# Second dense layer of three batches by one level of Strassen's method, in a fused attention and dense kernel on one Trainium2 core

## The chip, the cores and the metric

The kernel runs on one core of one Trainium2 chip. The metric is device time in microseconds (us) of one execution, the median of several runs. PE is TensorE, PEld its weight loads, DVE is VectorE, ACT is ScalarE, POOL is GpSimd; SP is SyncE, which issues transfers. In the chains of waits a q behind an engine's name (SPq) is its sequencer, and "issue" is time in which the engine waited for nothing that the profile shows.

Time before the change: 225.6 us median of the first three runs (225.41 to 226.26). Each experiment ran on the same chip as runs of the kernel before in between; x1 to x4, x5 to x8 and x9 to x11 ran on three different chips, where the kernel before had medians of 225.95, 225.98 and 225.92 us.

## The reference

Four batches of windowed attention with four sink tokens (8 heads, 768 tokens, head size 64), then a dense layer of 512 to 2048, relu squared, and a dense layer of 2048 to 512:

```python
scores = np.matmul(q, k.transpose(0, 1, 3, 2)) / np.sqrt(D)
keep = (pos[None, :] < n_sink) | ((rel >= 0) & (rel < window))      # 4, 128
a = softmax(np.where(keep, scores, -1e9))
x = np.matmul(a, v).transpose(0, 2, 1, 3).reshape(B * S, H * D)     # 3072 x 512
h = x @ w_in                                                        # 3072 x 2048
g = np.maximum(h, 0.0) ** 2
return g @ w_out                                                    # 3072 x 512
```

The dense layers are computed in bf16 with f32 sums.

## The kernel before

The kernel is written as operations with a key (a wished-for place), the engines that may run each and an estimated cost. A small planner in the kernel walks them when the program is built, takes the one that can start earliest and, among equals, the one with the smallest key, and emits it. The order on each engine is therefore fixed at build time, out of estimates.

```python
def layer1(b, key, fbs, c0, cw, need):          # first dense layer, relu, square
    ...
    ra = op(key, {"act": 0.19 + n * cw / 1200.0, "dve": 1.25}, relu, after=[a], takes=[rs], reads=[bs])
    def square(e):                              # gT = r * r: two SBUF inputs
        r = bank_t.pop((tag, "r"))
        (nc.vector if e == "dve" else nc.gpsimd).tensor_mul(
            gT_sb[c0 // 512][:, fbs[0]:fbs[0] + n, c0 % 512:c0 % 512 + cw], r, r)
    ops["sq", b, fbs[0], c0, cw] = op(key, {"dve": 0.7}, square, reads=[rs], after=[ra] + ...)

def layer2(b, u, keys, by_part=False):          # second dense layer, a pair of token tiles
    bs, os_ = Slot("den", 1), Slot("osb", 1)    # den: two 2-bank PSUM tiles
    ...
            def mm(e, i=i, t=t, part=part, n=n):
                if n == 0:
                    bank_t["y", b, u] = bank(bs, "py", [128, 2, DM], FP32)     # two PSUM banks
                ...
                for fb in range(4 * part, 4 * part + 4):                       # 16 per tile, 512 columns
                    nc.tensor.matmul(pm[:, i, :], lhsT=gT_sb[t // 4][:, fb, 128 * (t % 4):128 * (t % 4) + 128],
                                     rhs=w_out_sb[:, fb, :], start=(fb == 0), stop=(fb == NFB - 1))
    ...
    def evac(e):                                # one copy when the pair is complete
        o = bank_t["osb", b, u] = work["osb"].tile([128, 2, DM], FP32, name="osb", tag="osb")
        copy(e, o, bank_t["y", b, u])
    # ... one store on the SP queue; the last pair's second tile is copied in two halves, on ACT and DVE
```

A PSUM tile goes back to its pool when its evacuation has read it. Waits between engines are put in by the tile framework, from which instructions touched which tile.

The softmax here doesn't subtract the row's maximum and nothing guards it: scores larger than these inputs give would overflow.

Of the kernel before, what the change touches and what calls it, by code (L numbers as in the profile page):

```python
# [20 lines left out]
WARM_UNTIL = 34.0  # L21

# [10 lines left out]
class Op:  # L33
    def __init__(self, key, engines, run, after, takes, reads, dma, follow):
        self.key, self.engines, self.run = key, engines, run
        self.after, self.takes, self.reads, self.dma = list(after), list(takes), list(reads), dma
        self.follow, self.yields, self.margin = list(follow), [], 0.0
        self.end = self.issued = self.engine = None


class Plan:
# [8 lines left out]
    def __init__(self, capacity):  # L50
        self.ops, self.capacity = [], dict(capacity)

    def op(self, key, engines, run, after=(), takes=(), reads=(), dma=0.0, follow=()):
        o = Op(key, engines, run, after, takes, reads, dma, follow)
        self.ops.append(o)
        return o

    def run(self):
# [12 lines left out]
        while left:  # L71
            best = None
            for o in ready:
                t = 0.0
                need = {}
                for s in o.takes:
                    if len(s.pools) > 1:
                        s.pool = min(s.pools, key=lambda p: min(free[p], default=1e9))
                    need[s.pool] = need.get(s.pool, 0) + 1
                ok = True  # L80
                for p, n in need.items():
                    if len(free[p]) < n:
                        ok = False
                        break
                    t = max(t, sorted(free[p])[n - 1] + LATENCY)
                if not ok:
                    continue
                if o.dma:
                    past = landed.get(next(iter(o.engines)), ())
                    if len(past) >= 8:  # L90
                        t = max(t, past[-8])
                pick = None
                for e, c in o.engines.items():
                    slack = PE_SLACK if e == "pe" else 0.0
                    start = max([t + slack if t > 0 else 0.0, engine.get(e, 0.0)] +
                                [a.end + LATENCY + slack for a in o.after if a.engine != e or a.dma] +
                                [a.issued for a in o.follow])
                    if pick is None or start + c < pick[1] + pick[2]:
                        pick = (e, start, c)
                cand = (round(pick[1], 2), o.key)  # L100
                if best is None or cand < best[0]:
                    best = (cand, o, pick)
# [31 lines left out]
def kernel(  # L134
# [28 lines left out]
    sizes = dict(att=2, den=2, qr=5, qs=6, expm=8, r=3, osb=2)  # L163
# [9 lines left out]
    mask = consts.tile([128, 2, 4, 128], BF16)  # L173
    mask0 = consts.tile([128, 2, 4, 128], BF16)
    bias = consts.tile([128, 4, 128], BF16)
    bias0 = consts.tile([128, 4, 128], BF16)
# [10 lines left out]
    xT_sb = [consts.tile([128, NS, NKB, 256], BF16, name=f"xT{i}") for i in range(2)]  # L187
    gT_sb = [consts.tile([128, NFB, w], BF16, name=f"gT{i}") for i, w in enumerate((512, 256))]
# [63 lines left out]
    def build_masks(e):  # L252
        for h2 in range(2):
            for i in range(2):
                nc.gpsimd.tensor_copy(out=mask[:, h2, 2 * i:2 * i + 2, :], in_=tri)
                nc.gpsimd.tensor_copy(out=mask0[:, h2, 2 * i:2 * i + 2, :], in_=tri)
            nc.gpsimd.memset(mask0[0:NSINK, h2, 1:3, :], 1.0)
# [10 lines left out]
    c_fill = op(-9, {"dve": 2.5}, fill)  # L268
# [11 lines left out]
    def dma_op(queue, name, run, us, behind=None, takes=(), yields=()):  # L280

        def go(e):
            ds = run(e)
            if behind is not None:
                for d in ds:
                    after_dma(d, loaded[behind])
            loaded[name] = ds[-1]
        o = op(-5, {queue: (0.85 if queue == "pool" else 0.5) + (0.3 if behind else 0.0)}, go, dma=us, takes=takes,
               follow=[chained[queue]] if queue in chained else (),
               after=[ops[behind]] if behind is not None else ())  # L290
        ops[name] = chained[queue] = o
        o.yields += [ops[y] for y in yields]
        o.follow += [ops[y] for y in yields]
        return o

# [106 lines left out]
    def attention(b, key):  # L402
# [16 lines left out]
        def stage(g, f0, f1, side):  # L419

# [83 lines left out]
            if g == 0:  # L504
# [7 lines left out]
                def sink_values(e):  # L512
                    for j in range(NP):
# [9 lines left out]
                                    after=([ops["turn", b, 1, 0]] if b in NATURAL else copies) + prev_sinks)  # L523
            lo = max(256, t0)
# [20 lines left out]
            for s in range(t0 // 256, last // 256):  # L545
                fs = 0.36 + 0.5 * (256 * s - t0) / (last - t0)
                norms = []
                biased = b == 0 and s < BIASED
                for m0 in (0, 2):
# [27 lines left out]
                    for ms in ((m0,), (m0 + 1,)) if b == 0 else ((m0, m0 + 1),):  # L577
                        sc.append(op(
                            at(fm), {"pe": len(ms) * (0.7 if biased else 0.28) + 0.1}, lambda e, f=scores, ms=ms: f(e, ms),
                            takes=[banks[m - m0] for m in ms],  # L580
                            after=[ops["turn", b, ti, t] for ti in (0, 1)
# [5 lines left out]
                    for j, m in enumerate((m0, m0 + 1)):  # L587
# [7 lines left out]
                        def domask(e, s=s, m=m, o=o):  # L595
                            x = ex_t[b, s, m]
                            if e == "dve":
                                mk = (mask if s else mask0).rearrange("p h a c -> p h (a c)")
                                nc.vector.tensor_mul(x[:, :, o:512], x[:, :, o:512], mk[:, :, o:512])  # L599
                            elif s == 0:  # L600
                                mk = mask0.rearrange("p h a c -> p h (a c)")
                                nc.gpsimd.tensor_mul(x[:, :, o:512], x[:, :, o:512], mk[:, :, o:512])
# [12 lines left out]
                    bo = Slot(side, 1)  # L615

# [35 lines left out]
                    norms.append(op(at(fm + 0.17), {"dve": 0.95}, norm, after=[va] + prev_bridge, reads=[bo]))  # L652

# [30 lines left out]
    def layer1(b, key, fbs, c0, cw, need):  # L684
        n = len(fbs)
# [14 lines left out]
        def relu(e):  # L700
            r = bank_t[tag, "r"] = work["r"].tile([128, n, cw], BF16, name="r", tag="r")
            if e == "act":
                nc.scalar.activation(out=r, in_=bank_t.pop(tag), func=AF.Relu)  # L703
            else:
                nc.vector.tensor_scalar_max(r, bank_t.pop(tag), 0.0)
# [9 lines left out]
    def layer2(b, u, keys, by_part=False):  # L715

        tail = b == B - 1 and u == NS - 1
        bs = Slot("den", 1)
        bt_ = Slot("den", 1)
# [4 lines left out]
        for n, (i, part) in enumerate(order):  # L724
            t = 2 * u + i

            def mm(e, i=i, t=t, part=part, n=n):
                if n == 0:
                    bank_t["y", b, u] = bank(bs, "py", [128, 2, DM], FP32)
                if tail and n == 4:  # L730
                    bank_t["y", b, u, 1] = bank(bt_, "py", [128, 2, DM], FP32)
                pm = bank_t["y", b, u, 1] if tail and n >= 4 else bank_t["y", b, u]
                for fb in range(4 * part, 4 * part + 4):
# [5 lines left out]
                   takes=[bs] if n == 0 else [bt_] if tail and n == 4 else ())  # L739
# [9 lines left out]
        def store(e):  # L749
            nc.sync.dma_start(out=out[128 * g:128 * g + 256, :].rearrange("(i p) m -> p i m", p=128),  # L750
                              in_=bank_t.pop(("osb", b, u)))

        def evac_tail(i):
            def run(e):
                if i == 0:
                    bank_t["osb", b, u] = work["osb"].tile([128, 2, DM], FP32, name="osb", tag="osb")
                o, y = bank_t["osb", b, u], bank_t["y", b, u] if i == 0 else bank_t["y", b, u, 1]
                if i == 0:
                    copy("dve", o[:, 0, :], y[:, 0, :])
                    nc.sync.dma_start(out=out[128 * g:128 * g + 128, :], in_=o[:, 0, :])  # L760
                else:
                    h = work["qr"].tile([128, DM // 2], FP32, name="half", tag="qr")
                    copy("act", h, y[:, 1, 256:512])
                    copy("dve", o[:, 1, 0:256], y[:, 1, 0:256])
                    nc.scalar.dma_start(out=out[128 * g + 128:128 * g + 256, 256:512], in_=h)
                    nc.sync.dma_start(out=out[128 * g + 128:128 * g + 256, 0:256], in_=o[:, 1, 0:256])
            return run

        if tail:
            e0 = op(keys(0, 3), {"dve": 0.7}, evac_tail(0), after=[ops["layer2", b, 2 * u, 3]], takes=[os_], reads=[bs])  # L770
            op(keys(1, 3), {"dve": 0.5}, evac_tail(1), after=[a, e0], reads=[bt_, os_])
        else:
            ev = op(keys(1, 3), {"act": 1.05, "dve": 1.25}, evac, after=[a], takes=[os_], reads=[bs])
            op(keys(1, 3), {"sp": 0.1}, store, after=[ev], reads=[os_], dma=2.0)
# [32 lines left out]
    for b in range(B):  # L807
        if b == 0:
            at = attention(0, lambda f: f - 1.0)
            at(0, 0.0, 1.0, ("den", "att"))  # L810
            late["masks"] = op(0.006, {"pool": 3.0}, build_masks, after=[c_tri, ops["bridge", 0, 1]])
# [23 lines left out]
        for u in range(NS):  # L835
            if b == 0 and u < 2:
                layer2(b, u, lambda i, part, u=u: 0.408 + 0.466 * (4 * part + 2 * u + i) / 24, by_part=True)
            else:
                layer2(b, u, lambda i, part, u=u, b=b: b + 0.5 + 0.5 * (8 * u + 4 * i + part) / 24)
# [36 lines left out]
```

## Time and profile before

| | before |
|---|---|
| span of the profiled run | 223.8 us |
| PE busy | 215.5 us (96%) |
| DVE, ACT, POOL busy | 103.7, 115.9, 64.8 us |
| PE idle between 14.2 us and the last matmul | 1.8 us (205.67 us less PE's busy 203.84 in it) |
| last matmul to end of span | 3.9 us |

The page's opening lines and the chain of waits are shown in the prediction. Two more views matter later. First, PE's largest waits (who waited, for whom; us in total, times, longest), and the row of the mask multiplication, which like the squares reads two SBUF tiles (busy us, mean ns of one):

```profile
PE pt L201 <- POOL ident L239: 1.5, 1, 1.5
PE pt L476 <- DVE qs L208: 0.5, 1, 0.5
...
L599 DVE TENSOR_TENSOR expm<-expm,mask 128x1024 bf16<-128x1024 bf16 x27 | 18.9, 699 | 18.8 <-ACT expm L590 18.8
```

The reader is to see that PE hardly waits for anybody once the start is over (the 1.5 us fall before 14.2 us), and that DVE's mask row is at 699 ns and its square row (in the prediction) at 690, mostly with GpSimd issuing loads beside them. Why the mask row is 9 ns above the square row is taken up at the end.

### The profile page before, as it was taken

The numbers are of one execution on the slowest core, as the hardware profiler recorded it, in microseconds if no ns is written. First come the engines' busy times: TensorE is split into PE (matmuls) and PEld (weight loads), VectorE is DVE, ScalarE is ACT, GpSimd is POOL, SyncE is SP. The second block draws the span as 40 slices with busy tenths as digits, with TensorE's granted clock in tenths as the row PEclk, the third lists the DMA queues.
The fourth block names the chain that finished last, engine by engine and source line by source line (L and its number), as shares of the span: only waits on it lengthen the run. The fifth ranks groups of instructions, "written<-read, shape, count | busy, mean of one in ns | idle before, by whom it ended". The sixth has DMA issues, their size and how long they took to land.

```text
span 223.8 us, 4586 instructions
## 1 busy us (share of the span) xinstructions
PE 215.5 (96%) x1932; PEld 138.2 (62%) x1952; DVE 103.7 (46%) x192; ACT 115.9 (52%) x131; POOL 64.8 (29%) x99
## 2 busy tenths in 40 slices
PE   7899999999999999999999999999999999999993
PEld 7549996467865886555454545598464455874441
DVE  6646346476656764466452536657241024430010
ACT  2695566506893577286727188665351165551010
POOL 7991015055999415997100000000000000000000
PEclk9999999999999999999999999999999999999999
DMA  5999968998999999999999464020221320000222
GB/s 144 289 187 208 208 196 109 199 349 240 131 179 139 150 197 150 122 150 199 143 144 124 139 166 48 0 50 0 47 98 25 116 97 0 0 3 0 94 103 86
DMA packets 84309, 28.13 MB, mean 126 GB/s; under 512 B 70336, under 2 KB 80832, under 8 KB 84288
## 3 DMA queue, kind: packets, MB, share of 16 engines
q0 software_dynamic: 52608, 10.49, 61.9%
q1 hardware_dynamic: 31496, 17.20, 34.9%
q8 instruction: 15, 0.25, 0.4%
q10 hardware_dynamic: 184, 0.14, 0.2%
q14 instruction: 6, 0.05, 0.1%
HBM read 27.30 MB, written 6.29 MB: 150 GB/s over the span
## 4 chain that ended last, share of the span: by engine, by line
PE 91%; DMA 3%; SPq 2%; ACT 1%; DVE 1%; issue 1%; DVEq 0%
PE pm L694 38%; PE py L734 37%; PE po L634 6%; PE ps L571 5%; DMA qr<-in_q_dram 3%; PE pt L476 2%; SPq L348 2%; PE px L671 1%; DVE qkT L208 1%; PE ps L564 1%; PE pk L531 0%; ACT r L703 0%; ACT expm L590 0%; ACT qkT L206 0%; PE px L201 0%
## 5 line engine op out<-in xcount | busy, mean ns | idle before, releaser
L734 PE MATMUL py<-w_out_sb,gT 128*128 128x512 bf16 x366 | 86.1, 379 | 1.1 <-issue 0.3
L694 PE MATMUL pm<-xT,w_in_sb 128*128 128x256 bf16 (+1 forms) x576 | 86.7, 308 | 0.4 <-ACT r L703 0.3
L694 PEld LDWEIGHTS <-w_in_sb 128*128 128x128 bf16 x576 | 63.0, 114 | 20.9 <-issue 1.7
L703 ACT ACTIVATE r<-pm 128x1024 bf16<-128x1024 f32 x48 | 49.2, 1025 | 32.7 <-PE pm L694 23.9
L734 PEld LDWEIGHTS <-gT 128*128 128x128 bf16 x384 | 35.4, 98 | 39.2 <-issue 1.7
L710 DVE TENSOR_TENSOR gT<-r 128x1024 bf16<-128x1024 bf16 x48 | 33.1, 690 | 50.3 <-ACT r L703 50.2
L590 ACT ACTIVATE expm<-ps 128x1024 bf16<-128x1024 f32 (+1 forms) x48 | 43.2, 952 | 17.1 <-PE ps L571 17.1
L599 DVE TENSOR_TENSOR expm<-expm,mask 128x1024 bf16<-128x1024 bf16 (+1 forms) x39 | 25.4, 654 | 23.7 <-ACT expm L590 23.2
L206 ACT ACTIVATE osb<-py 128x1024 f32<-128x1024 f32 x9 | 9.2, 1024 | 31.2 <-PE py L734 31.1
L634 PEld LDWEIGHTS <-expm 128*128 128x128 bf16 x352 | 16.5, 97 | 4.1 <-issue 0.6
L634 PE MATMUL po<-v,expm 128*128 128x65 bf16 x352 | 17.5, 193 | 0.0
L646 DVE TENSOR_TENSOR xn_sb<-po,rc 128x512 bf16<-128x512 f32 x24 | 16.6, 691 | 0.8
L571 PE MATMUL ps<-qkT 64*128 64x128 bf16 (+1 forms) x256 | 14.8, 238 | 0.3
L571 PEld LDWEIGHTS <-qkT 64*128 64x128 bf16 x256 | 8.0, 94 | 10.7 <-issue 9.9
L634 PE MATMUL po<-vs,es 128*128 128x65 bf16 x128 | 13.1, 193 | 0.0
L208 DVE COPY osb<-py 128x1024 f32<-128x1024 f32 (+2 forms) x4 | 3.6, 889 | 19.0 <-PE py L734 15.9
L210 POOL CAST qs<-qr 128x512 bf16<-128x512 f32 x6 | 4.2, 714 | 26.2 <-DVE gT L710 14.1
L634 PEld LDWEIGHTS <-es 128*128 128x128 bf16 x128 | 11.7, 97 | 0.0
L390 POOL DMA_DIRECT2D v<-in_v_dram x12 | 10.8, 918 | 3.4 <-DMA qn<-in_q_dram 2.5
L380 POOL DMA_DIRECT2D qn<-in_q_dram x12 | 10.8, 918 | 1.5 <-DMA qn<-in_k_dram 1.2
L361 POOL DMA_DIRECT2D v<-in_v_dram x12 | 10.9, 926 | 0.5 <-DMA qr<-in_k_dram 0.5
L208 DVE CAST qs<-qr 128x512 bf16<-128x512 f32 x16 | 8.1, 513 | 6.2 <-DMA qr<-in_k_dram 3.1
(51 smaller groups left out, 108.1 us busy)
## 6 DMA issues: line engine op xcount, KB each, us to landing
out_dram<-osb SPq DMA_DIRECT2D x11, 512.0 KB, 2.8
v<-in_v_dram POOLq DMA_DIRECT2D x24, 128.0 KB, 6.5
qr<-in_k_dram SPq DMA_DIRECT2D x8, 256.0 KB, 5.2
qr<-in_q_dram SPq DMA_DIRECT2D x8, 256.0 KB, 4.9
w_in_sb<-in_moe_w_in_dram POOLq DMA_DIRECT2D x4, 512.0 KB, 9.8
w_out_sb<-in_moe_w_out_dram POOLq DMA_DIRECT2D x4, 512.0 KB, 10.8
qn<-in_k_dram POOLq DMA_DIRECT2D x12, 128.0 KB, 7.2
qn<-in_q_dram POOLq DMA_DIRECT2D x12, 128.0 KB, 8.8
```

Source lines behind the costliest of these rows:

```text
L208: nc.vector.tensor_copy(out=dst, in_=src)
L361: return [nc.gpsimd.dma_start(out=v_sb[b % 2][:, t, :, 0:D], in_=v[b, :, 128 * t:128 * t + 128, :].rearrange("h p d -> p h d"))]
L380: return [nc.gpsimd.dma_start(out=qn_t[b, ti][:, t, :].rearrange("p (h d) -> p h d", d=D), in_=(q, k)[ti][b, :, 128 * t:128 * t + 128, :]. ...
L571: nc.tensor.matmul(ps[:, h2, o:o + w], lhsT=qkT_sb[r, m, 1, c, :], rhs=qkT_sb[r, m, 0, qb:qb + w // 128, :], start=(i == 0 and not biased) ...
L590: nc.scalar.activation(out=x[:, :, o:512], in_=bank_t["s", b, s, m][:, :, o:512], func=AF.Exp, scale=scale)
L599: nc.vector.tensor_mul(x[:, :, o:512], x[:, :, o:512], mk[:, :, o:512])
L634: nc.tensor.matmul(pv[:, i, h2, :], lhsT=lhsT, rhs=rhs, start=(n_ == 0), stop=(n_ == len(mms) - 1))
L646: nc.vector.tensor_tensor(out=xn_sb[:, 2 * s:2 * s + 2, 128 * m0:128 * m0 + 256].rearrange("p i (j h d) -> p j i h d", j=2, d=D), in0=pv[: ...
L694: nc.tensor.matmul(pm[:, i, :], lhsT=w_in_sb[:, fb // 4, kb, fb % 4:512:4], rhs=xT[:, c0 // 256:(c0 + cw) // 256, kb, :], start=(kb == 0), ...
L703: nc.scalar.activation(out=r, in_=bank_t.pop(tag), func=AF.Relu)
L710: (nc.vector if e == "dve" else nc.gpsimd).tensor_mul(gT_sb[c0 // 512][:, fbs[0]:fbs[0] + n, c0 % 512:c0 % 512 + cw], r, r)
L734: nc.tensor.matmul(pm[:, i, :], lhsT=gT_sb[t // 4][:, fb, 128 * (t % 4):128 * (t % 4) + 128], rhs=w_out_sb[:, fb, :], start=(fb == 0), sto ...
```

## The change

Its intent: for batches 1 to 3, write each pair of token tiles (256 tokens x 2048 by 2048 x 512) as a 2 x 2 block product, and compute it with seven half-size products instead of eight. The price is four sums of activation blocks per pair, four sums of weight blocks once, and more evacuations, since the seven products are combined in SBUF and PSUM. The pair's tiles become the even and odd tokens, so that one store per pair still works. Keys of the order are shifted and stretched per stage (`PLACES`). Some mask tiles are smaller.

```diff
+    ("l2", 1): (0.08, 0.78), ("l2", 2): (-0.09, 1.47), ("l2", 3): (-0.37, 0.8), ...   # PLACES, 31 entries
+    def place(self, places):
+        ... o.key = first[o.group] + shift + (o.key - first[o.group]) * scale
     def relu(e):
-                nc.scalar.activation(out=r, in_=bank_t.pop(tag), func=AF.Relu)
+                nc.scalar.activation(out=o, in_=h, func=AF.Relu)      # h: even, then odd tokens
+    def weight_sums(key, after):            # B12-B11, B22-B12, B22-(B12-B11), B21-...
+            last = [op(key, {"dve": 1.3, "pool": 2.5}, run, ...)]
+    def layer2_fast(b, u, key):
+        def total(name, x, y, how, slot, n_key, after, reads):
+            ...
+                (nc.vector if e == "dve" else nc.gpsimd).tensor_tensor(
+                    out=t_[name], in0=..., in1=..., op=how)
+            return op(n_key, {"dve": 0.72, "pool": 1.35}, run, after=after, ...)
+        o1 = total("s1", a21, a22, ALU.add, ...)        # s3 = a11-a21, s2 = s1-a11, s4 = a12-s2
+        bs, os_, us = Slot("den", 1 if tail else 2), Slot("osb", 1), Slot("u", 1)
+        def region(name):                   # quarters of one py tile: c, b in bank 0; d, a in bank 1
+            h, part = {"c": (0, 0), "b": (0, 1), "d": (1, 0), "a": (1, 1)}[name]
+            return bank_t["y", b, u][:, h, part, :]
+        p5 = product(0, "c", "s1", 1, True, ...)        # each: 8 matmuls of 256 columns
+        p7 = product(1, "d", "s3", 3, True, ...)
+        x0 = taken("x", "c", os_, 0, [p5])              # copy of quarter c, in mid-pair
+        p1 = product(2, "a", a11, w(0, 0), False, ...)
+        p6 = product(3, "b", "s2", 2, False, ...)
+        u0 = taken("u", "a", us, 2, [p1])
+        ex = pair_sum("x", "d", 2, [x0, p1])            # x += d, from PSUM
+        p3 = product(4, "c", "s4", w(1, 1), False, ...)
+        p4 = product(5, "d", a22, 4, False, ...)
+        eu = pair_sum("u", "b", 4, [u0, p3])
+        ...                                             # x += u; p2 into a; sum of 512; copy of a; store
         for u in range(NS):
+            else:
+                layer2_fast(b, u, lambda n, u=u, b=b: b + 0.5 + 0.5 * (8 * u + 8 * n / 7.0) / 24)
+    P.place(PLACES)
     P.run()
```

## The prediction

> **What bounds the kernel now.** I read the table of busy times first, then the chain of waits (what ended last, followed back), then the groups of instructions by shape, then a table of busy times by stage. The page opens:
>
> ```profile
> span 223.8 us, 4586 instructions
> PE 215.5 (96%) x1932; PEld 138.2 (62%) x1952; DVE 103.7 (46%) x192; ACT 115.9 (52%) x131; POOL 64.8 (29%) x99
> PE 91%; DMA 3%; SPq 2%; ACT 1%; DVE 1%; issue 1%; DVEq 0%
> PE pm L694 38%; PE py L734 37%; PE po L634 6%; PE ps L571 5%; DMA qr<-in_q_dram 3%; PE pt L476 2%; SPq L348 2%; PE px L671 1%; DVE qkT L208 1%; PE ps L564 1%; PE pk L531 0%; ACT r L703 0%; ACT expm L590 0%; ACT qkT L206 0%; PE px L201 0%
> ```
>
> The reader is to see that 91% of the last chain is TensorE, and 37 points of it the second dense layer (py, L734), which the change rewrites. A busy PE need not be a PE at its peak, so I checked the spacing of the matmuls in the chain, where each piece is start, length, what:
>
> ```profile
> 20.76 14.13 PE pm L694 x128
> 118.11 3.56 PE py L734 x16
> 168.03 10.31 PE py L734 x47
> 178.33 20.80 PE pm L694 x128
> 199.13 0.22 PE py L734
> 199.40 10.74 PE py L734 x49
> 210.19 9.67 PE py L734 x44
> 219.87 0.02 issue
> ```
>
> The last batch's second layer has 96 matmuls of 512 columns and runs from 199.13 to 219.87: 20.74 us, 0.216 us each (the counts x49 and x44 fall short because some records are missing). Batch 0's first layer is 128 matmuls of 256 columns in 14.13 us, 0.110 each; 20.80 us for 64 of 512 and 64 of 256 fits the same two rates (64 x 0.216 + 64 x 0.109). So **half the columns cost half the time, plus about 2%**, though each matmul has its own weight load. The stage table gives PE busy 43.28 of 43.80 us, 36.29 of 37.00, 49.79 of 50.00, 32.74 of 33.00 between 14.2 and 178 us: 1.7 us idle in 164. PE is the bound, and PE time saved there is time saved.
>
> **What the Trainium skill says.** "TensorE: Matmul & The Clock Gate", section Back-to-back issue gap, gives N/2.4 + 2.5 ns for a warm gap: 216 ns at 512 columns, 109 at 256. The trace agrees (216, 110). The same section's sustained 131 ns at 512 columns does not: this trace shows 216. "VectorE: DVE Perf Modes", section The perf-mode tier table: tensor_tensor gets twice the base rate with bf16 in SBUF, the base rate with a PSUM operand. The trace agrees:
>
> ```profile
> L710 DVE TENSOR_TENSOR gT<-r 128x1024 bf16<-128x1024 bf16 x48 | 33.1, 690 | 50.3 <-ACT r L703 50.2
> L646 DVE TENSOR_TENSOR xn_sb<-po,rc 128x512 bf16<-128x512 f32 x24 | 16.6, 691 | 0.8
> L208 DVE COPY osb<-py 128x256 f32<-128x256 f32 x1 | 0.4, 425 | 3.1 <-ACT half L206 3.1
> L206 ACT ACTIVATE half<-py 128x256 f32<-128x256 f32 x1 | 0.4, 383 | 5.9 <-PE py L734 5.9
> ```
>
> 1024 bf16 elements cost what 512 from PSUM cost, 0.69 us: these are the prices for the added sums and evacuations. "PSUM — Partial Sum Buffer", section PSUM bank collisions raise a hardware error: two engines may not be in one bank and quadrant at once, so the new evacuations in mid-pair must be waited for by PE. The old kernel evacuates only after a pair is complete, so its trace does not show this. "SBUF — State Buffer", section Who interferes with whom: a DVE instruction with two SBUF inputs contends with a GpSimd instruction that reads SBUF. No overlap in the old trace isolates it.
>
> **The change, part by part.** The built instruction orders show which engine got what.
>
> 1. PE, second layer of batches 1 to 3. Removed: 3 batches x 6 tiles x 16 matmuls of 512 columns = 288 x 0.216 = 62.2 us. Added: 3 batches x 3 pairs x 7 products x 8 matmuls of 256 columns = 504 x 0.110 = 55.4 us. On the path: **-6.8 us**. (The order has 416 more PE rows: 216 matmuls more with their loads, less 8 warm-up ones.) The gain is 1/8 of 62.2, 7.8 us, less 1.0 us for the 2% dearer half-width matmul.
>
> 2. Sums of activations, four per pair, 36 in all. The order puts 23 on DVE (23 x 0.69 = 15.9 us) and 13 on GpSimd. Sums of weights: four of 2048 bf16 elements, all on DVE; twice the elements of the square, so about 1.3 us each (estimate from the 690 ns row), 5 us once, near the end of batch 0.
>
> 3. Evacuations. A pair was one copy of 1024 f32 (ACT 1.02 us). Now it is two copies of 256 (0.38 ACT or 0.43 DVE), two adds from PSUM of 256 (0.43), one add of 256 in SBUF (0.43), one add of 512 from PSUM (0.69), one copy of 256 (0.43): 2.8 us, about 2.0 of it on DVE. Nine pairs: DVE +18 to +20, ACT roughly level. Together DVE gains some 40 us: 103.7 becomes 140 to 150 of a shorter span, 65 to 69%. All beside PE unless a stage is denser than the mean.
>
> 4. Relu now reads PSUM with stride two, so that a pair's tiles are even and odd tokens. Strided PSUM reads already run at full rate: ACT's strided copy qkT of 512 elements took 595 ns, its contiguous exponential es of 512 took 592. I charge 0.
>
> 5. Moved order. The early warm-up matmuls fall from 72 to 64: those in front of the second px are gone, and the first layer of the first 256 tokens goes ahead of it. In the old chain 8 and 10 warm-up matmuls (0.45 and 0.56 us) stood on the path while PE waited for the norms. I take **-0.5 us**.
>
> 6. The end. After the last matmul (219.87) the old kernel copies 256 columns on ACT, then 256 on DVE (0.39 + 0.42, one after the other). Now it is 128 and 128: by the slopes between the rows of 256 and of 1024 or 512 elements, 0.28 + 0.29. **-0.2 us**.
>
> 7. New waits. Within a pair PE waits for up to four evacuations, but at least one other product of 8 x 0.11 = 0.88 us lies between the product read and the next write to its bank, against 0.4 us of copy. In the last batch I walked the order by hand: sums stand ready 1 to 2 us before their products, except the last pair's on GpSimd, which are about in time. What stays is the 0.05 us of "issue" that the old chain shows behind a py start that waited, for some third of 63 products (1 us), and a few exposed sums or masks, as DVE is nearly full (about 85% by my count of the order) around batch 1's first layer. I take **+1.5 us**.
>
> Sum: -6.8 - 0.5 - 0.2 + 1.5 = -6.0. From 225.6 that is **219.6 us**, 2.7% less.
>
> **Rivals.**
>
> *DVE becomes the bound in a stage.* The stage from 95 to 145 us has DVE at 26.6 of 50 us; batch 1's share of sums and evacuations (13 to 15 us) makes it about 41. For: masks, norms and squares on DVE stand in PE's path with only two pairs of banks each for attention and dense work. Against: the order was set with these costs, and keys shifted per stage look like a search for an order without stalls. If it bites: 3 to 5 us of PE gaps, 221 to 223 us, "same".
>
> *GpSimd's sums come late.* The only GpSimd tensor_tensor in the old trace, 130 f32 elements, took 463 ns; its bf16 copies of 256 and 512 took 394 and 609, hence a fixed 0.18 and, for two inputs, 2.2 ns per element: 2.4 us for 1024 elements, against the 1.35 the new kernel's plan writes down. And DVE may be locked out meanwhile. Against: only 13 sums, most with slack; bf16 may be cheaper than f32. Worst case 13 x 1 us, of which perhaps 2 us on the path: 221.5 us.
>
> *Half-width matmuls run slower than 0.110* because weight loads (97 ns for gT rows, 114 for w_in) just fit under 109. If 0.120, 504 x 0.010 = 5 us and nearly all the gain goes: 224.6. Against: pm at 256 columns ran at 0.109 to 0.114 with the slower, strided loads; the new loads read contiguous columns.
>
> *All hidden and the search found more:* waits under 0.5 us, start better by 1 us: 217.5 us.
>
> **Range and chances.** The -6.8 is firm to half a microsecond; waits may be 0.5 to 4.5 us, the start may be off by 0.7 either way. Range 217.3 to 222.6. The 2% line is 221.1, 1.5 us above the prediction: passed if waits exceed 3 us. Faster 0.77, same 0.21, slower 0.02.
>
> **What would show it.** Step 1: the last batch's products at 0.109 to 0.112 us per matmul in the chain; py rows of 256 columns x504 minus missing records. Steps 2 and 3: DVE busy 140 to 150 us, ACT 112 to 117, sums at 0.69 on DVE and 1.3 to 2.4 on GpSimd. Step 4: relu still about 1.025 us. Step 5: PE's dense stream starts near 20 us or a little sooner. Step 6: last matmul to end of span 3.7 us. Step 7: idle PE time between 14 us and the last matmul of 2 to 4 us against 1.8. Wrong if PE's idle time exceeds 5 us with DVE named as releaser, if relu or masks got slower through strides and broadcasts, or if transfers of batch 2 and 3 come later because GpSimd issues them behind sums.

## The result

The changed kernel takes **252.5 us** (median of 4 runs, 251.82 to 253.5) against 225.93 (225.41 to 226.43) of the kernel before in the same rounds. The ratio is 1.118, 95% interval 1.115 to 1.122: slower by 12%. Ratios here and below are the mean time of one kernel's fast runs over the mean of the other's fast runs of the same rounds, so not quite the ratio of the medians quoted. Executions over 1.5% slower than the fastest of the same kernel are left out of the means.

The page after the change: span, busy times, granted TensorE clock by slice (tenths), and the chain of waits by engine.

```profile
span 251.8 us, 5147 instructions
...
PE 220.1 (87%) x2160; PEld 162.0 (64%) x2160; DVE 162.3 (64%) x267; ACT 113.6 (45%) x138; POOL 94.9 (38%) x104
...
PEclk9999999999999999998599999967999999959999
...
PE 64%; DVE 23%; issue 4%; ACT 3%; DMA 2%; SPq 1%; DVEq 0%
```

PE's share of the last chain fell from 91% to 64%, and DVE has 23% of it. Yet PE's busy time rose by 4.6 us although an eighth of the second layer's work in three batches is gone; the clock row has slices at 0.5 to 0.8 that the old one, all 9, did not have. DVE is busy for 162 us, not the 140 to 150 foretold. PE's waits:

```profile
PE ps L597 <- DVE xn_sb L676: 7.9, 3, 3.8
PE py L861 <- DVE osb L882: 6.2, 7, 0.9
PE py L861 <- DVE sg L828: 2.5, 1, 2.5
PE py L861 <- DVE u L882: 2.1, 4, 0.5
PE po L664 <- DVE expm L630: 2.0, 1, 2.0
```

Two patterns stand out. The waits for `osb` and `u` are many and equal: 0.9 us seven times, 0.5 us four times, about once per pair. The others are few and long, up to 3.8 us. PE is idle for 24.2 us from 14.2 us to the last matmul, against 1.8 before (here and below: the length of that window less PE's busy time in it).

**The long waits.** The groups by shape (busy us, mean ns of one) show which DVE rows grew:

```profile
L745 DVE TENSOR_TENSOR gT<-r 128x1024 bf16<-128x1024 bf16 x48 | 38.9, 812 | 27.5 <-ACT r L738 27.5
L828 POOL TENSOR_TENSOR gT<-gT 128x1024 bf16<-128x1024 bf16 x6 | 13.7, 2287 | 18.0 <-DVE sg L828 17.7
L898 DVE TENSOR_TENSOR osb<-osb,u 128x256 f32<-128x256 f32 x9 | 11.6, 1294 | 0.3
L630 DVE TENSOR_TENSOR expm<-expm,tri 128x1024 bf16<-128x1024 bf16 x26 | 18.8, 740 | 6.0 <-ACT expm L617 6.0
```

Squares, unchanged instructions, went from 690 to 812 ns; an f32 add of 256 columns takes 1294 ns. All the stretched rows read two SBUF tiles. One GpSimd sum takes 2.3 us. The timeline of DVE, GpSimd and PE from 111 us on (start, us, engine, what) shows one such stretch whole:

```profile
111.87 2.13 POOL L828 TENSOR_TENSOR gT<-gT 128x1024 bf16<-128x1024 bf16 x1
...
111.90 5.42 DVE L898 TENSOR_TENSOR osb<-osb,u 128x256 f32<-128x256 f32 x1
...
114.90 2.13 POOL L828 TENSOR_TENSOR gT<-gT 128x1024 bf16<-128x1024 bf16 x1
...
117.47 0.69 DVE L676 TENSOR_TENSOR xn_sb<-po,rc 128x512 bf16<-128x512 f32 x1
...
118.22 0.61 PE L597 MATMUL ps<-qkT 64*128 64x128 bf16 x6 [3.06 <-DVE xn_sb L676]
```

The add is recorded as lasting from just after one GpSimd sum began until just after the next one ended: 5.42 us. Behind it on DVE stands the norm `xn_sb`, which empties a PSUM bank that PE's next scores need; PE waits 3.06 us. The chain of waits names `xn_sb`, which itself took its usual 0.69 us; the culprit stands ahead of it in DVE's queue. GpSimd was not free between the two sums: from 113.95 to 114.87 us it issued a load.

**The short waits.** A piece of the chain in the last pairs (start, us, what):

```profile
234.27 1.76 PE py L861 x16
236.06 0.42 DVE u L231
236.48 0.34 DVE osb L882
236.87 1.92 PE py L861 x16
```

PE stops after two products until DVE has copied `u` out of quarter a and added quarter d to `osb`, and only then starts p3, which writes quarter c. It needs neither: quarter c was copied long before, and d and a lie in another bank. In the built program, p3's wait points at that add, p1's at the copy of c, and the copy of c itself waits for p7 in the other bank. The trace agrees on the last: the first pair's copy of c starts at 105.24 us, after 16 of its matmuls, and not after p5's 8. The waits are per `py` tile, which spans two banks, and not per quarter or bank.

**The clock.** After 4 us of gaps between 115 and 120 us the chain has

```profile
120.39 4.99 PE py L861 x24
```

which is 0.208 us per 256-column matmul instead of 0.110. The mean granted clock is 0.93 from 95 to 145 us and 0.90 from 145 to 178 us, against 1.00 in both stretches before. The mean clock of the whole run, 0.958, comes to some 10.6 us of 251.8 (an estimate from these two figures).

### The profile page after: what moved, and what is told of

Its sections match the earlier page's. It is cut to its first block, busy times and chain, and to the rows that moved or that the text cites. A ratio compares the mean times of both kernels' runs of the same rounds, so it can differ in the third digit from the quotient of the medians.

```text
span 251.8 us, 5147 instructions
## 1 busy us (share of the span) xinstructions
PE 220.1 (87%) x2160; PEld 162.0 (64%) x2160; DVE 162.3 (64%) x267; ACT 113.6 (45%) x138; POOL 94.9 (38%) x104
## 3 DMA queue, kind: packets, MB, share of 16 engines
q1 hardware_dynamic: 30232, 17.27, 30.2%
## 4 chain that ended last, share of the span: by engine, by line
PE 64%; DVE 23%; issue 4%; ACT 3%; DMA 2%; SPq 1%; DVEq 0%
PE pm L727 28%; PE py L861 19%; PE py L765 7%; DVE gT L745 5%; PE po L664 4%; DVE osb L898 3%; PE ps L597 3%; DVE sg L828 3%; DMA qr<-in_q_dram 2%; DVE wt L800 2%; DVE qkT L231 2%; DVE osb L882 1%; DVE xn_sb L676 1%; SPq L372 1%; DVE expm L630 1%
## 5 line engine op out<-in xcount | busy, mean ns | idle before, releaser
L738 ACT ACTIVATE r<-pm 128x1024 bf16<-128x1024 f32 x48 | 49.1, 1026 | 50.6 <-PE pm L727 46.7
L745 DVE TENSOR_TENSOR gT<-r 128x1024 bf16<-128x1024 bf16 x48 | 38.9, 812 | 27.5 <-ACT r L738 27.5
L828 POOL TENSOR_TENSOR sg<-gT 128x1024 bf16<-128x1024 bf16 x4 | 9.3, 2334 | 76.4 <-DVE gT L745 67.0
L861 PEld LDWEIGHTS <-sg 128*128 128x128 bf16 x216 | 21.7, 102 | 14.2 <-issue 8.0
L765 PE MATMUL py<-w_out_sb,gT 128*128 128x512 bf16 x96 | 23.2, 380 | 0.0
L861 PE MATMUL py<-wt,sg 128*128 128x256 bf16 x144 | 20.1, 286 | 3.3 <-DVE sg L828 2.5
L630 DVE TENSOR_TENSOR expm<-expm,tri 128x1024 bf16<-128x1024 bf16 x26 | 18.8, 740 | 6.0 <-ACT expm L617 6.0
L861 PE MATMUL py<-wt,gT 128*128 128x256 bf16 x144 | 20.4, 289 | 0.7 <-DVE gT L828 0.7
L828 POOL TENSOR_TENSOR gT<-gT 128x1024 bf16<-128x1024 bf16 x6 | 13.7, 2287 | 18.0 <-DVE sg L828 17.7
L861 PE MATMUL py<-w_out_sb,gT 128*128 128x256 bf16 x128 | 17.8, 287 | 2.5 <-DVE u L882 2.1
L861 PE MATMUL py<-w_out_sb,sg 128*128 128x256 bf16 x72 | 10.1, 287 | 5.5 <-DVE osb L882 5.5
## 6 DMA issues: line engine op xcount, KB each, us to landing
w_out_sb<-in_moe_w_out_dram POOLq DMA_DIRECT2D x4, 512.0 KB, 10.8
```

Source lines behind the costliest of these rows:

```text
L630: nc.vector.tensor_mul(y, y, tri.rearrange("p (o a) c -> p o (a c)", o=1).to_broadcast([128, 4, 256]))
L738: nc.scalar.activation(out=o, in_=h, func=AF.Relu)
L745: (nc.vector if e == "dve" else nc.gpsimd).tensor_mul(gT_sb[c0 // 512][:, fbs[0]:fbs[0] + n, c0 % 512:c0 % 512 + cw], r, r)
L828: (nc.vector if e == "dve" else nc.gpsimd).tensor_tensor(out=t_[name], in0=x if not isinstance(x, str) else t_[x], in1=y if not isinstance ...
L861: nc.tensor.matmul(y, lhsT=x[:, i, :], rhs=w_[:, i, :], start=first and i == 0, stop=i == HB - 1, skip_group_check=not first)
```

## The experiments

Two theories of the loss: L (GpSimd's sums hold DVE's two-input instructions; "the lock" below) and W (waits on the whole `py` tile). A rival is that DVE simply has too much work, whoever does what. Eleven kernels ran, all with correct results.

### x1: the sums on DVE

```diff
-                (nc.vector if e == "dve" else nc.gpsimd).tensor_tensor(
+                nc.vector.tensor_tensor(                    # in total(): same place in the order
```

> The changed kernel with one edit: the 13 activation sums that GpSimd did are issued on DVE, at the same places of the program. Theory L (GpSimd's two-input sums hold DVE's second read path, so DVE's two-input operations stretch to 1.3 to 5.4 us and PE idles behind them, about 13.5 of its 24 us of idle time, plus about 10 us at a lowered TensorE clock after the long gaps): 226 to 232 us, DVE tensor_tensor rows back at 0.69 us, no PE gap over 1.5 us. Theory W (the waits between products and evacuations in one PSUM tile are the main cost): the lock is secondary, 244 to 250 us. Theory D (DVE simply has too much work): 13 more sums on DVE make it worse or equal, 250 us or more.

Measured: 233.99 us (233.27 to 234.3), ratio 1.036 [1.032, 1.039]. PE's idle time fell from 24.2 to 11.5 us; what is left are nearly all short waits. PE's two largest waits, and the add's row, in this kernel:

```profile
PE py L861 <- DVE osb L882: 6.6, 7, 1.3
PE py L861 <- DVE u L882: 2.1, 4, 0.5
...
L898 DVE TENSOR_TENSOR osb<-osb,u 128x256 f32<-128x256 f32 x9 | 3.8, 424 | 0.3
```

The add fell from 1294 to 424 ns and the squares to 689. Thirteen sums more on DVE made DVE's busy time fall, 162.3 to 147.5 us. So DVE was not short of throughput; it was being held. The time missed the expected interval by 2 us on the slow side; that the short waits weigh more than I had thought is likely, but not shown apart. Theory L explains 18.5 of the 26.6 us lost, but not all.

### x2: waits between banks taken away

The matmuls and the evacuations of different banks of one pair are declared independent; those of the same bank still wait.

```diff
+        BANK = dict(c=0, b=0, d=1, a=2 if tail else 1)
+        def writes(m, name):
+            for x, r in read:
+                if BANK[x] != BANK[name]:
+                    tc.declare_no_dep(m.ins, r.ins, reason="another bank")
+            wrote.append((name, m))
+        ...                                  # and the same from the evacuations' side
```

> The changed kernel, sums on GpSimd kept, but each product and each evacuation of a Strassen pair now waits only for the others of its own PSUM bank, no longer for the whole two-bank tile ([...]the semaphores inside a bank stay). Theory L: the six gaps of 0.93 us and four of 0.51 us behind L882 go, about 7.6 us, the GpSimd gaps stay: 243 to 248 us. Theory W: 235 us or less.

Measured: 243.58 us (241.41 to 246.18), ratio 1.070 [1.067, 1.074]. Two of the four runs are slow; the two fast ones, 241.41 and 242.09 us, lie 0.9 to 1.6 us below the interval that theory L gave, and 6 us above that of theory W. The profile is of the fastest. The first line of PE's waits, and the add's row:

```profile
PE ps L597 <- DVE xn_sb L676: 8.6, 3, 3.8
...
L912 DVE TENSOR_TENSOR osb<-osb,u 128x256 f32<-128x256 f32 x9 | 12.4, 1378 | 0.3
```

The waits of `py` for `osb` and `u` are gone from the list; the long ones stay, and so does the stretched add. PE's idle time is 17.3 us, 6.9 less than in the changed kernel. Each experiment takes away its own pattern and leaves the other.

### x3: both

> Both edits together. If GpSimd's sums and the whole-tile waits together are what the prediction missed, PE's idle time after 14 us comes down to 2 to 5 us and the time to 219 to 223 us. If something else of the change costs (strided relu, broadcast masks, order), it stays above 226 us.

Measured: **222.44 us** (221.34 to 223.01), ratio 0.984 [0.981, 0.988]. It is faster than both kernels, than the one before by 1.6% with an interval clear of 1. Its page:

```profile
span 219.5 us, 5139 instructions
...
PE 209.3 (95%) x2160; PEld 158.6 (72%) x2160; DVE 147.5 (67%) x280; ACT 113.3 (52%) x138; POOL 64.9 (30%) x91
...
PE 82%; DVE 5%; ACT 4%; DMA 3%; issue 2%; SPq 2%; DVEq 0%; ACTq 0%
```

PE is the bound again. Its idle time is 2.7 us, and its busy time 6.2 us below that of the kernel before. Apart, the two parts save 18.5 us (x1) and 10.8 (x2, mean of its two fast runs, 241.75); together they save 30.1. That is the sum of both, 29.3, within the spread of the runs.

### x4: the side changes without Strassen

All of the change's other edits stay (even and odd tokens, smaller masks, order of the start), the products are the plain ones, and the keys are not shifted, as they were found for other work.

```diff
-                layer2_fast(b, u, lambda n, u=u, b=b: ...)
+                layer2(b, u, lambda i, part, u=u, b=b: b + 0.5 + 0.5 * (8 * u + 4 * i + part) / 24)
-    P.place(PLACES)
+    P.place({})
```

> The changed kernel with Strassen undone and the keys not shifted: the ordinary products in all batches, but the changed relu (strided read), the paired rows of the output, the broadcast masks and shorter mask building kept; the last pair is evacuated whole. If these side changes cost nothing, 225 to 228 us (the tail is about 1 us longer). If they are part of the loss, 230 us or more.

Measured: 229.31 us (228.84 to 230.95), ratio 1.017 [1.012, 1.021]. This falls between the two expected intervals, and against the 2% line it is unclear. No DVE row is stretched (squares 691, masks 690 and 557 ns) and PE waits for no evacuation, so the big loss comes with the Strassen part. The profiled run is the slowest of the four, with a span of 229.2 us, 5.4 more than the kernel before. In it one gap of 1.4 us (scores waiting for an exponential at 130.6 us) is followed by 16 matmuls of 512 columns in 5.26 us instead of 3.46, and the end is 0.7 us longer; these make 3.9 us, and the rest was not traced. The other three runs have clocks of 0.998 to 0.999 and are still 2.9 to 3.6 us above the kernel before. Which side edit, or which change of order, costs this was not tried.

### x5 and x6: GpSimd's sums alone, and a control that only writes

To the kernel *before*, whose PE and ACT orders stay identical and whose DVE order gains one mask that the planner moved over from GpSimd (the same in x5 and x6), twelve GpSimd instructions are added into a tile that nobody reads: in x5 sums of two `gT` blocks, in x6 memsets of the same length.

```diff
+                for n in range(2 if u == 0 else 1) if b else ():
+                    op(..., {"pool": 2.3}, lambda e, g=g: nc.gpsimd.tensor_tensor(      # x5
+                           out=scr..., in0=g[:, 0:8, 0:128], in1=g[:, 8:16, 128:256], op=ALU.add), ...)
+                    # x6 instead: nc.gpsimd.memset(scr, 0.5), 2560 columns
```

> The kernel before, its PE, DVE and ACT orders untouched, plus twelve GpSimd sums of 1024 bf16 elements of the activations (four per batch 1 to 3, once the squares exist) into a tile nobody reads. Theory L (the port): each takes 2.1 to 2.6 us, DVE's squares and masks beside them stretch from 0.69 to 2 us or more, and though nobody waits for the sums, PE gets gaps: 229 to 238 us. Rival (late sums hurt only because products wait for them): 225.5 to 227 us, DVE rows stay at 0.69.

> Control for the run before: twelve GpSimd memsets of about 2 us each at the same places of GpSimd's order (they wait for no data, so most run as soon as the loads are issued, about 95 to 145 us), which write SBUF and read nothing. If it is reading through the shared path that holds DVE: DVE's rows stay at 0.69 us and the time at 225.5 to 227.5 us. If any busy GpSimd slows DVE: as in the run before.

Measured: x5 232.39 us (230.08 to 233.7; of the three fast runs 232.08), ratio 1.026 [1.020, 1.031]; x6 227.67 us (227.36 to 228.85), ratio 1.009 [1.006, 1.013]. The groups of x5 and PE's largest wait in it:

```profile
L712 DVE TENSOR_TENSOR gT<-r 128x1024 bf16<-128x1024 bf16 x48 | 40.3, 842 | 46.2 <-ACT r L705 46.2
L845 POOL TENSOR_TENSOR scr<-gT 128x1024 bf16<-128x1024 bf16 x12 | 26.8, 2234 | 86.0 <-DVE gT L712 82.3 <-DVE rc L647 3.3
...
PE po L636 <- DVE expm L601: 4.1, 4, 2.5
```

The groups of x6:

```profile
L712 DVE TENSOR_TENSOR gT<-r 128x1024 bf16<-128x1024 bf16 x48 | 33.2, 691 | 49.0 <-ACT r L705 48.9
L845 POOL MEMSET scr<- 128x2560 bf16 x12 | 26.9, 2243 | 0.4
...
L510 DVE COPY kblk<-qkT 64x16 bf16<-64x16 bf16 x8 | 6.6, 820 | 0.7 <-ACT qkT L208 0.7
```

GpSimd is busy just as long in both, 26.8 and 26.9 us. Under the sums DVE's squares and masks stretch and DVE's busy time grows by 14.6 us (103.7 to 118.3), of which 0.7 is the mask that moved; under the memsets those rows stay at 691. The memsets ran at other times than the sums, so I looked which rows they met: in x5 five squares and four masks overlap a sum and take 2150 and 2576 ns on average, the others 690 and 699; in x6 six squares and eight masks overlap a memset and take 689 and 690. Three norms `xn_sb`, which read one PSUM and one SBUF tile, overlap sums in x5 and stay at 692. The lock is therefore in what GpSimd reads, not in GpSimd being busy. This is what the Trainium skill says under "SBUF — State Buffer", section Who interferes with whom, and here it is measured. The control was not free: the one-input copy `kblk` went from 208 to 820 ns (two of eight took 2.1 and 3.0 us, beside GpSimd's load issues and memsets), and one gap of 1.5 us opened behind them. The same section lists copies among the instructions that can contend with GpSimd in a 2-port mode; whether this copy runs in one, no run here shows. So x6 came out just above the interval I had written.

### x7 and x8: the keys

x7 is x3 with the keys not shifted (`P.place({})`). x8 is x3 with the planner told that sums, weight sums, last quarters and first masks are for DVE alone, with the shifted keys kept, so that it finds its own order around that.

```diff
-            return op(n_key, {"dve": 0.72, "pool": 1.35}, run, after=after,        # x8, and three like it
+            return op(n_key, {"dve": 0.72}, run, after=after,
```

> The version with both edits (sums on DVE, waits by bank), but with the keys of the order not shifted: what the shifted keys are worth by themselves. If they only fit a plan that had the costs of GpSimd wrong: within 1 us of the version with both edits, 221 to 224 us. If they are needed to keep DVE-heavy stages off PE's path: 225 to 230 us.

> The version with both edits, the order planned anew with the true choice of engines (no two-input GpSimd operation in any batch: sums, first-stage masks, last quarter all on DVE), keys shifted as in the changed kernel. DVE gets about 3 us more than in the version with both edits, without the GpSimd masks that held it. 219.5 to 222.5 us if the plan's order was the rest of the loss; 222.5 or more if not.

Measured: x7 227.83 us (227.25 to 230.0), ratio 1.011 [1.005, 1.016]; x8 226.61 us (225.7 to 227.93), ratio 1.004 [1.000, 1.008]. PE is idle for 8.2 us in x7 and 6.6 us in x8, in gaps of 0.9 to 1.5 us that name DVE sums, a copy or an exponential in turn. So the shifted keys are worth 5.4 us to x3, and they do not carry over to another order: letting the planner decide again with better facts gave 4.2 us back. With unshifted keys on both sides, Strassen's products alone are worth 229.31 - 227.83 = 1.5 us; the two ratios' intervals, 1.012 to 1.021 and 1.005 to 1.016, overlap, so this gain is not clear of noise.

### x9 to x11: the last masks, and the end

x9 is x3 with the two remaining two-input GpSimd instructions, masks of a batch's first stage, on DVE at the same places. x10 also issues the last pair's two larger stores ahead of the last quarter's. x11 is x3 again, for the same rounds.

```diff
-                                (nc.vector if e == "dve" else nc.gpsimd).tensor_mul(y, y, mk)     # x9, x10
+                                nc.vector.tensor_mul(y, y, mk)
+            store_rest()                     # x10: in first_quarter, ahead of the copies
```

> The kernel with the sums on DVE and the bank waits removed (222.44 us), and besides it the two masks of a batch's first stage that GpSimd had now also written on DVE at the same places; nothing else changes. Theory L (a GpSimd instruction that reads SBUF holds DVE's two-input instructions): no DVE row stretches any more, the two-input mask row falls from 730 to about 695 ns, and PE's idle time falls from 2.7 us to 2.0 to 2.7; 221.0 to 222.5 us. Rival: DVE is the scarce engine and two more masks of 0.56 us on it come onto the path, 222.5 to 224 us.

> The same, and the last pair's two other stores issued on the SP queue ahead of the last quarter's store instead of after it (their data are ready about 0.8 us sooner). Theory T (the tail of the changed kernel is one issue after the other on one queue, 3 x 0.4 us): last matmul to end of span falls from 4.9 to 4.0 to 4.3 us, and the time by 0.5 to 0.9 us against the kernel without it. Rival: the stores' own time of landing sets the end and not their issue, and then the 128 x 128 quarter, issued last, ends as late as before: within 0.2 us.

> The kernel with the sums on DVE and the bank waits removed once more, unchanged, to have it in the same rounds as the two above: 222.0 to 222.9 us, 0.982 to 0.987 of before.

Measured, against before at 225.92 (225.47 to 226.43): x9 222.88 us (221.28 to 223.76), ratio 0.986 [0.983, 0.989]; x10 223.25 us (222.6 to 223.81), 0.987 [0.985, 0.989]; x11 222.21 us (221.89 to 222.73), 0.984 [0.982, 0.986]. Both edits did what they were meant to do locally: the mask row of 768 elements fell from 728 to 553 ns, and in x10 the end shrank from 4.9 to 4.2 us. Neither made the kernel faster, so both time expectations missed; x9's 222.88 us even lies in the interval of its rival, that two more masks on DVE come onto the path, though PE's list shows no wait for them (its one new wait, 0.9 us, names a GpSimd cast). One reason shows in the chain of waits: the same 16 matmuls at the same place in the program, in x9 and then in x11.

```profile
65.54 3.25 PE pm L727 x16
```

```profile
65.28 1.87 PE pm L727 x16
```

In both runs three short waits (0.3 to 0.6 us each) lie just ahead. In x9 the clock then fell (0.71 between 66 and 70 us), in x11 it stayed at 1.00. That costs x9's profiled run 1.4 us, and x10's shows the same (0.62 in that stretch). Whether a run meets it changes from run to run: x11's four runs show mean clocks of 0.987 to 1.000. In x10, at clock 1.0, one run still had a span of 220.6 against 220.1 and 220.2 in x11, so the 0.7 us saved in the end do not show there, and where they went is not settled.

## Why the prediction was wrong, step by step

The spans of the profiled runs grew by 28.0 us, 223.8 to 251.8. With x3 as the measure of what the change does without the two waits, it splits thus:

| term | predicted | measured | from |
|---|---|---|---|
| PE's work (step 1) | -6.8 | -6.2 | PE busy 215.5, in x3 209.3 |
| end (step 6) | -0.2 | +1.2 | last matmul to end 3.9, after 5.1 |
| start (step 5) | -0.5 | -0.2 | what is left of the 28.0 |
| new waits (step 7), all of PE's idle time | +1.5 | +22.4 | idle 1.8, after 24.2 |
| slower clock | not in the sum | +10.8 | PE busy 209.3 in x3, 220.1 after |

- **Step 1** was right (x3's own mean clock is 0.994, so the -6.2 is not quite at full clock). The half-width products run at 0.109 us per matmul where the clock is full, and the rival of slow half-width matmuls is out. From x3's chain:

```profile
204.14 6.11 PE py L875 x56
```

- **Steps 2 and 3** were right in counts and in single durations (step 3's own durations add up to 3.2 us a pair, not the 2.8 written there): sums of 0.69 us on DVE, weight sums of 1.22 (1.3 estimated), GpSimd's sums 2.1 to 2.6 us (2.4 estimated). DVE's busy time without the lock is 147.5 us in x3, with 13 sums (9.0 us) that the prediction had on GpSimd; like for like that is 138.5, just under the range foretold.
- **Step 4** was right: relu takes 1026 ns as before.
- **Step 5** has the right sign and can't be read off cleanly: the remainder is -0.2 us, while the dense stream starts 0.9 us sooner, at 19.87 instead of 20.76; the eight warm-up matmuls that are gone count under PE's work.
- **Step 6** had the wrong sign. I counted the copies and not the stores behind them: the SP queue issues three stores one after the other behind the last copy, 0.33, 0.44 and 0.42 us in x3. x10 confirms the size: issued earlier, the end shrinks by 0.7 us.
- **Step 7 failed, and it decided the outcome:** +22.4 us instead of +1.5. It failed in two places, and the larger one, the lock, is the next point (12.7 us of idle time gone in x1); the smaller one is the wait per tile. "At least one other product of 8 x 0.11 = 0.88 us lies between the product read and the next write to its bank" is true of the banks and beside the point: the program waits per tile, and a pair has one tile for both banks. The order alone would have shown it, had I looked up which instruction each wait names instead of reasoning from the bank map. x1, where only these waits are left, puts 8.7 us of gaps on them, about 0.9 and 0.5 us per pair.
- **The second rival had the right mechanism and the wrong size.** "DVE may be locked out meanwhile" stands there, and then I charged only the lateness of the sums themselves: "13 x 1 us, of which perhaps 2 us on the path". What counts is what stands behind the held instruction in DVE's queue. The thirteen sums last 30.2 us; DVE's busy time is 162.3 us with them and 147.5 without, although x3's figure has 13 sums of 0.69 us more in it. So 14.8 + 9.0, some 24 us of 30, went into holding DVE (an estimate from these figures). Taking the lock away (x1) removed 12.7 us of idle time. I wrote that no overlap in the old trace isolates it, and then set it near zero; unknown should have widened the range. And the old trace did hold a hint, which I overlooked:

```profile
86.11 1.22 POOL L222 TENSOR_SCALAR_AFFINE_SELECT expm<-expm 128x512 bf16<-128x512 bf16 x2 [6.54 <-ACT expm L590]
86.98 0.89 DVE L599 TENSOR_TENSOR expm<-expm,mask 128x1024 bf16<-128x1024 bf16 x1 [0.29 <-ACT expm L590]
87.30 1.30 POOL L514 TENSOR_TENSOR vs<-vs_in,head_rows 32x130 bf16<-32x130 f32 x2
```

This is the only mask or square of the old kernel that ran beside GpSimd arithmetic on SBUF, and it took 0.89 us instead of 0.69; the ones beside GpSimd's load issues did not stretch. It alone lifts the row's mean of 27 from about 692 to 699 ns. One stretched row of 0.2 us gives no size for a GpSimd sum of 2.3 us, but it says that the cost is not zero.

- **The slower clock** appears nowhere in the prediction, and cost +10.8 us. Gaps of 2 to 4 us were paid for twice here, once as idle time and once as matmuls at half the rate after them (0.208 us instead of 0.110 behind the gaps at 115 to 120 us).
- **The first rival, DVE as the bound**, is refuted for this order by x1: more sums on DVE, less DVE time, and 18.5 us gained. In x3 PE is busy for all of the 50 us from 95 to 145 us, where the rival was placed, with DVE at 35.3 us. In the orders of x7 and x8, gaps of 0.9 and 1.4 us do name a DVE sum.

What stays open: what x4's 3.4 us are made of, why a DVE add stays held while GpSimd issues a load between two sums, and why x10's shorter end does not show in its time. The two causes of the loss are shown, each by its own undoing and the lock also by adding it to the kernel before.

## What to carry to other kernels

When work moves to GpSimd, ask not whether GpSimd has time, but whether DVE runs two-input instructions on SBUF meanwhile, and who waits for what stands behind them in DVE's queue. When an accumulator is read in mid-computation, look at which instruction each wait in the built program names; a tile that spans two banks makes waits between banks that the data do not need. And count every gap of a few microseconds of TensorE twice, because the matmuls after it may run at half the rate, as they did here (0.208 us instead of 0.110); an order tuned on estimates is worth keeping only with the facts that it was tuned for.

## What the Trainium skill lacked or had wrong

- "SBUF — State Buffer", section Who interferes with whom: the rule is right (squares 842 ns beside GpSimd's sums, 691 beside memsets), but it says that the other side is blocked for the whole instruction. Here a DVE add of 0.42 us was held over two GpSimd sums and the 0.9 us between them, in which GpSimd issued a load, 5.42 us; the section says nothing of being held over several instructions.
- "TensorE: Matmul & The Clock Gate", section HAM oscillation — how this bites in real kernels: the rule given is no idle gap above about 3.4 us. In x9 no gap near the stretch was above 0.62 us, with PE busy for 2.52 of 4.00 us (62 to 66 us), and the clock of the next 4 us fell to 0.71; in x11 PE was busy for 2.18 of the same 4.00 us and the clock stayed at 1.00. The section after it speaks of short idle times without a number.
- The same page, section Back-to-back issue gap: the sustained 131 ns at 512 columns is not met; this trace has 216 ns, as the section's own formula says.
- I found no page that says at what grain the waits of a tile are put in (here the whole two-bank tile, 0.9 and 0.5 us per pair), nor one with the cost of issuing several stores in a row from one queue (0.33 to 0.44 us each here).
